# The third load of x goes from SyncE's queue to ScalarE's, ahead of two small vectors

## The chip, the cores and the metric

The kernel runs on one core of a Trainium2 chip. A core has five engines with a program each: TensorE (PE, with PEld for its weight loads), VectorE (DVE), ScalarE (ACT), GpSimd (POOL) and SyncE (SP). Engines that issue transfers do so in the order of their own program, and an issue can wait, which holds up all that stands behind it on that engine. The transfers themselves run on 16 DMA engines of the core. The metric is the device time of one execution in microseconds (us); lower is better.

## The reference

The input x has 2048 tokens of 1024 values. Three things are computed from it:

```python
g = sigmoid((x * gate_w).sum(-1, keepdims=True))          # a gate for each token
X = rfft2(x) * (w_r + 1j * w_i);  a = irfft2(X)           # a filter in the frequency domain
dt = exp(log_dt);  Lam_bar = exp(dt * (Lambda_re + 1j * Lambda_im))
Bu = x @ (((Lam_bar - 1) / Lam)[:, None] * (B_re + 1j * B_im)).T
h[t] = Lam_bar * h[t - 1] + Bu[t]                         # a complex scan over all 2048 tokens
b = 2 * (h @ (C_re + 1j * C_im).T).real + x * Dskip
out = g * a + (1 - g) * b
```

The five vectors Lambda_re, Lambda_im, log_dt, Dskip and gate_w have 1024 values each (2 KB). The first three are needed for the scan's coefficients, Dskip and gate_w later.

## The kernel before, in words

Everything is one program with its order written out by hand. The stages are generators (one for each kind of step), and a long string, `ORDER`, names a generator per letter: the program is emitted by stepping the generators in that order, and each engine runs its own instructions in the order in which they were emitted. Nothing is rearranged afterwards.

**Loads.** x is viewed as 128 partitions by 16 row groups of 1024 values and lands in the storage that later holds the matrix C (tile `CT`; `xn[i]` is its i-th part, with two row groups). `load_x` (letter `x`, line 242) makes the first two row groups two loads of 256 KB, called a and b below, and then one load of 512 KB for each further pair: c (row groups 2 and 3, i = 1), d, e, f and g; the last four row groups come by transposing loads (line 238). All of these are issued by SyncE, and so are the tables: `G` in three pieces (line 252, the matrices of the first Fourier step), `T2` in three pieces (line 247, those of the second), `JP` (line 1027), and the matrix B by transposing loads (line 259, letter `b`, tile `BT`). SyncE's order at the start is: a, b, c, the three pieces of G, d, two pieces of T2, e, JP, f, a transpose of B, g, a transposing load of x, and so on. The five small vectors are loaded at the very start by ScalarE on its own queue (line 211), into the rows of one tile, `vec8`.

**Completion semaphores.** The loads that SyncE and ScalarE issue take their completion semaphores in turn from a set of eight, in the order of emission over both queues. A load that gets a semaphore waits, on the engine that issues it, until the load that had it before has landed. So the ninth load waits for the first, and a load on one queue can wait for one on the other.

**What uses the first loads.** TensorE starts with seven idle matmuls on zeros (line 987), then transposes the row groups one after the other, eight 128 x 128 transposes each (`turn`, line 919, out of `CT` into a PSUM tile `pt`). The first three small vectors are turned between the first and the second row group (`turn_vectors`, line 1080). Ahead of row group 2, the first of load c, stand 22 filler transposes of the identity (line 917, `FILL_T`). Behind row group 2 stand the two late vectors (`turn_late_vectors`, line 1097), then row group 3, then the first matmuls of the Fourier step (`fd`, lines 433 and 443, against `G`). ScalarE copies each transposed row group to `xQ` (`turn_out`, line 929). Before its first copy it loads its function table; it then works out the coefficients of the scan (lines 1086 to 1113), takes over the late vectors (lines 1099 and 1100), and goes on with copies of row groups and of Fourier results (line 449). The second Fourier step on TensorE is line 462 (against `T2`), and ScalarE takes its results at line 474. VectorE folds the copied row groups (lines 943 to 954) and makes tables for the scan. The products of x with B (line 398) feed the scan from about 30 us on.

Of the kernel before, what the change touches and what calls it, by code (L numbers as in the profile page):

```python
# [24 lines left out]
P = 128  # L25
# [117 lines left out]
def kernel(  # L143
# [17 lines left out]
    nc = tc.nc  # L161
# [45 lines left out]


    vec8 = tmp.tile([8, 5, P], BF16, name="vec8")
    for i, src in enumerate((B_Lambda_re, B_Lambda_im, B_log_dt, B_Dskip, gate_w)):  # L210
        nc.scalar.dma_start(out=vec8[:, i, :], in_=src.rearrange("(j p) -> j p", p=P))
    ident = cpool.tile([P, P], BF16, name="ident")
    make_identity(nc, ident)
# [11 lines left out]
    xn = [CT[i // 4][:, 2 * (i % 4):2 * (i % 4) + 2, :] for i in range(8)]  # L225
    x_v = x.rearrange("(p j) d -> p j d", j=16)
# [7 lines left out]
    def load_x():  # L234
        for i in range(8):
            if i >= NTURN // 2:
                g = i - NTURN // 2
                nc.sync.dma_start_transpose(out=xt[:, :, :, g].rearrange("p j d s -> p (j d) s"), in_=x_sg[g][:, NTURN * D:])
                yield
                continue  # L240
            for js in (slice(0, 1), slice(1, 2)) if i == 0 else (slice(0, 2),):
                nc.sync.dma_start(out=xn[i][:, js], in_=x_v[:, 2 * i + js.start:2 * i + js.stop, :])
                yield

    def load_T2():
# [916 lines left out]
    def once(f):  # L1162
# [5 lines left out]
        "V": turn_vectors(), "|": turn_late_vectors(), "T": turn(), "U": turn_out(), "f": fold(), "~": mirror(), "u": fold_odd(), "F": fd(), "E": fd_out(), "S": s1(), "A": s1_out(), "1": s1_store(),  # L1168
        "K": keep_A1(), "h": unit_mm(), "H": unit_out(), "t": chain(*(make_tab(jp) for jp in range(4))), "r": radii(), "a": small(),
        "g": once(gate), "e": gate_out(), "b": load_B(), "c": load_C(), "2": load_T2(), "x": load_x(), "G": load_G(), "w": load_Wcols(), "k": load_turns(),  # L1170
        "n": early_mm(), "N": early_out(), "J": early_store(), "s": middle(), "L": load_small(), "M": load_mid(), "W": load_W(),
        "3": s2(), "4": s2_out(), "j": unit_cols(), "5": times_w(), "6": is1(), "7": is1_out(), "8": is1_store(), "q": load_last(), "i": is2(), "I": is2_out(),
# [43 lines left out]
```

## Time and profile before

| | |
|---|---|
| Time, median of 3 runs | 305.36 us (305.14 to 306.62) |
| The profiled execution's own time | 305.35 us |
| Its span in the profile | 303.6 us |
| Busy: TensorE / VectorE / ScalarE / GpSimd | 98% / 95% / 62% / 24% |
| Mean granted TensorE clock | 0.999 of full speed |

A row of a timeline has the start in us from the span's start, the length in us, the engine, the line, the operation, the tiles written and read, and xN for N merged instructions; square brackets tell how long the engine was idle before it and what ended that. SPq and ACTq are the queues of SyncE and ScalarE: their rows are the issuing of transfers, not the transfers. A row of waits has the waiting engine and line, what it waited for, the time in total, how often, and the longest. In the DMA view q1 is SyncE's queue and q10 ScalarE's. A row of windows has for each engine (PE, PEld, DVE, ACT, POOL) the busy time in that stretch, then the granted clock, the mean busy share of the DMA engines and GB/s.

### The profile page before, as it was taken

What the parts mean: (1) busy time and instruction counts of PE and PEld (TensorE: products, weight loads), DVE (VectorE), ACT (ScalarE), POOL (GpSimd) and SP (SyncE); (2) the same over time, 40 slices, a digit from 0 to 9 for tenths busy, and PEclk for the clock granted to TensorE, in tenths of its full rate; (3) what the DMA queues carried; (4) which work ended last, traced back from release to release, by engine and by line L of the source; (5) the groups of instructions that cost most, each with busy time, mean ns of one, the idle gap of its engine ahead of it and who ended that gap; (6) DMA issues with size and microseconds to landing.
All of it is one profiled execution on the core that took longest, in us unless ns stands there. A gap on an engine that the chain in (4) does not pass through costs nothing. (4 is left out here: it accounts for less than half of the span.)

```text
span 303.6 us, 6402 instructions
## 1 busy us (share of the span) xinstructions
PE 296.4 (98%) x2568; PEld 197.4 (65%) x2592; DVE 289.3 (95%) x340; ACT 188.5 (62%) x255; POOL 73.3 (24%) x99
## 2 busy tenths in 40 slices
PE   8999999999999999999999999999999999999995
PEld 5664677878864685458553866669657986645543
DVE  2999999999999999999999999999899999999995
ACT  4999999896532383667665865529668774343400
POOL 2100420745893001110210220202011253252330
PEclk9999999999999999999999999999999999999999
DMA  6999999989999599895948798687758876978976
GB/s 208 341 201 194 253 193 310 162 142 154 268 214 241 160 259 219 181 250 189 212 96 258 163 223 225 139 294 147 242 174 185 165 88 135 160 132 143 165 153 181
DMA packets 74157, 59.35 MB, mean 196 GB/s; under 512 B 44904, under 2 KB 61680, under 8 KB 74128
## 3 DMA queue, kind: packets, MB, share of 16 engines
q1 hardware_dynamic: 66560, 49.82, 65.8%
q0 software_dynamic: 6912, 8.69, 23.0%
q10 hardware_dynamic: 656, 0.44, 0.5%
q8 instruction: 20, 0.33, 0.4%
q14 instruction: 9, 0.07, 0.1%
HBM read 27.46 MB, written 23.08 MB: 166 GB/s over the span
## 5 line engine op out<-in xcount | busy, mean ns | idle before, releaser
L398 PE MATMUL psu<-xQ,BT 128*128 128x256 bf16 x1024 | 116.5, 273 | 0.2 <-DVE X L449 0.2
L398 PEld LDWEIGHTS <-BT 128*128 128x128 bf16 x1024 | 99.0, 98 | 17.3 <-issue 4.6
L713 PE MATMUL ps_y<-CT,h 128*128 128x512 bf16 x397 | 92.5, 379 | 0.9
L363 DVE TENSOR_TENSOR_SCAN h<-rz,h 128x2048 bf16<-128x2048 f32 (+1 forms) x20 | 70.8, 3561 | 0.0
L713 PEld LDWEIGHTS <-h 128*128 128x128 bf16 x416 | 39.6, 98 | 46.3 <-issue 2.9
L785 POOL DMA_DIRECT2D y_scratch<-su x20 | 17.3, 902 | 135.7 <-ACT su L779 105.4
L408 ACT CAST h<-psu 128x1024 bf16<-128x1024 f32 x32 | 32.3, 1011 | 18.7 <-PE psu L398 13.1
L350 DVE TENSOR_TENSOR h<-h,tab 128x4096 bf16<-128x4096 bf16 (+1 forms) x20 | 37.1, 1859 | 0.1
L744 ACT ACTIVATE ye<-ps_y,omg 128x512 f32<-128x512 f32 x26 | 17.9, 689 | 26.3 <-PE ps_y L713 11.8
L347 DVE TENSOR_TENSOR xQ<-h,tab 128x4096 bf16<-128x4096 bf16 x12 | 27.4, 2284 | 1.0 <-ACT h L408 1.0
L603 ACT CAST X<-ps_s 128x1024 bf16<-128x1024 f32 x16 | 16.2, 1010 | 14.6 <-PE ps_s L594 11.2
L727 PE MATMUL ps_q<-CT,h 128*128 128x512 bf16 (+2 forms) x110 | 21.3, 348 | 0.2
L817 ACT ACTIVATE BT<-ps_id,gB 128x1024 bf16<-128x1024 f32 x14 | 15.3, 1114 | 9.9 <-PE ps_id L810 5.7
L671 ACT CAST ZT<-ps_is 128x1024 bf16<-128x1024 f32 x16 | 15.8, 1017 | 6.2 <-PE ps_is L661 6.2
L637 ACT CAST C<-ps_is 128x1024 bf16<-128x1024 f32 x16 | 15.7, 1011 | 5.1 <-DMA xQ<-in_A_x_dram 3.4
L851 POOL DMA_DIRECT2D BT<-y_scratch x10 | 13.1, 1452 | 19.7 <-DVE BT L846 13.3
L727 PEld LDWEIGHTS <-h 128*128 128x128 bf16 x112 | 10.3, 98 | 10.4 <-DVE h L378 0.5
L779 ACT ACTIVATE su<-xs,omg 128x512 f32<-128x512 bf16 x20 | 14.2, 723 | 4.1 <-DMA y_scratch<-su 2.2
L929 ACT COPY xQ<-pt 128x1024 bf16<-128x1024 bf16 x12 | 12.2, 1082 | 1.3 <-PE pt L919 1.3
L449 ACT CAST X<-ps_fd 128x1024 bf16<-128x1024 f32 x12 | 12.3, 1062 | 1.0 <-PE ps_fd L439 0.9
L617 DVE TENSOR_TENSOR UV<-X,Wb 128x2048 bf16<-128x2048 bf16 x8 | 9.6, 1220 | 0.6 <-ACT ye L744 0.6
L617 DVE TENSOR_TENSOR UV<-X,raw 128x2048 bf16<-128x2048 bf16 x8 | 9.8, 1223 | 0.2 <-ACT X L604 0.2
(200 smaller groups left out, 397.3 us busy)
## 6 DMA issues: line engine op xcount, KB each, us to landing
y_scratch<-ye SPq DMA_DIRECT2D x20, 256.0 KB, 4.6
y_scratch<-su POOLq DMA_DIRECT2D x20, 256.0 KB, 4.7
Bb<-turn_scratch SPq DMA_DIRECT2D x16, 256.0 KB, 5.2
turn_scratch<-C SPq DMA_DIRECT2D x16, 256.0 KB, 4.1
raw<-turn_scratch SPq DMA_DIRECT2D x8, 512.0 KB, 4.3
xs<-in_A_x_dram SPq DMA_DIRECT2D x13, 256.0 KB, 3.9
out_dram<-BT SPq DMA_DIRECT2D x11, 256.0 KB, 4.3
CT<-in_A_x_dram SPq DMA_DIRECT2D x5, 512.0 KB, 6.1
```

The source lines that it names most:

```text
L347: nc.vector.tensor_mul(out=tmps["s"], in0=u[:, ::-1], in1=bc(i))
L350: nc.vector.tensor_mul(out=u, in0=u, in1=bc(i))
L363: nc.vector.tensor_tensor_scan(out=seg, data0=rz[:, js.start + j:js.start + j + m].rearrange("p j t -> p (j t)"), data1=seg, initial=0.0, ...
L398: nc.tensor.matmul(psu[:, j, :], lhsT=BT[4 * q + j][:, ri, d8, :], rhs=xQ[:, c, d8, :], start=(d8 == 0), stop=(d8 == 7))
L408: nc.scalar.copy(out=hs[c][:, ri, 4 * q:4 * q + 4].rearrange("p b (q j) -> p b q j", j=32), in_=psus.pop((c, q, ri)).rearrange("p b (j q) ...
L603: nc.scalar.copy(out=X2, in_=ps2s[g][b])
L617: nc.vector.tensor_mul(out=UV, in0=X2s.pop((g, b)).unsqueeze(1).to_broadcast([P, 2, 2, K]), in1=fft["Wb"][g // 2 % 2][:, :, at:at + 1, :]. ...
L671: nc.scalar.copy(out=ZT[:, 4 * kp:4 * kp + 4, :, 4 * G:4 * G + 4].rearrange("p (c r) n g -> p c r n g", c=2), in_=pszs.pop((G, kp)).rearra ...
L713: nc.tensor.matmul(psy, lhsT=hs[c][:, ri, jb, P * tq:P * (tq + 1)], rhs=CT[ri][:, jb, 512 * dh:512 * (dh + 1)], start=(i == 0), stop=(i == ...
L727: nc.tensor.matmul(psq, lhsT=hs[c][:, ri, jb, P * tq:P * (tq + 1)], rhs=CT[ri][:, jb, at:at + n], start=(i == 0), stop=(i == 15))
L744: nc.scalar.activation(out=ye, in_=psys[tb][:, K * hf:K * (hf + 1)], func=ACT.Copy, scale=omg[:, tb:tb + 1])
L785: nc.gpsimd.dma_start(out=y_dram[tb, hf], in_=xgs[tb, hf], accum_op=ALU.add)
```

## The change

Load c (row groups 2 and 3) is issued by ScalarE. It stands after Lambda_re, Lambda_im and log_dt, and the loads of Dskip and gate_w, which were issued directly after these, now follow load c. All loads have the same sources, destinations and sizes. ScalarE's order at the start is: Lambda_re, Lambda_im, log_dt, load c, Dskip, gate_w, the table load; SyncE's is: a, b, the three pieces of G, d, and on as before.

Because load c and the two vectors change places in the order of emission, the turns of the eight semaphores shift for the first loads: Dskip now waits for Lambda_re and gate_w for Lambda_im; the second piece of G waits for nothing and the third for load a; d waits for b and the first piece of T2 for log_dt, as before; the second piece of T2 waits for load c (Dskip before), e for the first piece of G (c before), JP for the second piece of G (gate_w before), f for Dskip (the first piece of G before), the first transpose of B for the third piece of G (the second before), and g for gate_w (the third piece of G before). From there on the waits are as they were.

```diff
     vec8 = tmp.tile([8, 5, P], BF16, name="vec8")
-    for i, src in enumerate((B_Lambda_re, B_Lambda_im, B_log_dt, B_Dskip, gate_w)):
+    vecs = list(enumerate((B_Lambda_re, B_Lambda_im, B_log_dt, B_Dskip, gate_w)))
+    for i, src in vecs[:3]:
         nc.scalar.dma_start(out=vec8[:, i, :], in_=src.rearrange("(j p) -> j p", p=P))
...
             for js in (slice(0, 1), slice(1, 2)) if i == 0 else (slice(0, 2),):
-                nc.sync.dma_start(out=xn[i][:, js], in_=x_v[:, 2 * i + js.start:2 * i + js.stop, :])
+                (nc.scalar if i == 1 else nc.sync).dma_start(out=xn[i][:, js], in_=x_v[:, 2 * i + js.start:2 * i + js.stop, :])
+                if i == 1:
+                    for k, src in vecs[3:]:
+                        nc.scalar.dma_start(out=vec8[:, k, :], in_=src.rearrange("(j p) -> j p", p=P))
                 yield
```

## The prediction

> **What bounds the kernel now.** I read the page first, then the timelines of SyncE's queue, ScalarE and TensorE over the first 30 us, the waits of SyncE's queue, the DMA landings in narrow stretches, and the one-microsecond windows. The change touches only the first 12 us, so the question is what limits that stretch and what it hands on.
>
> ```profile
> span 303.6 us, 6402 instructions
> PE 296.4 (98%) x2568; PEld 197.4 (65%) x2592; DVE 289.3 (95%) x340; ACT 188.5 (62%) x255; POOL 73.3 (24%) x99
> ...
> ACT  4999999896532383667665865529668774343400
> ```
>
> Over the whole span TensorE (98%) and VectorE (95%) are both full, so a delay handed on from the start has little idle time in which to vanish: 7.2 us on TensorE, 14.3 us on VectorE. One slice of the digits is 7.6 us: ScalarE, only 62% busy on average, is full from 8 to 53 us. The first stage is ScalarE's. SyncE's queue (duration is the issue time, xN the merged issues):
>
> ```profile
> 0.73 1.34 SPq L242 DMA_DIRECT2D CT<-in_A_x_dram  x3
> 2.12 2.06 SPq L252 DMA_DIRECT2D G_sb<-c_G  x3
> 4.22 0.72 SPq L242 DMA_DIRECT2D CT<-in_A_x_dram  x1
> 4.98 2.09 SPq L247 DMA_DIRECT2D raw<-c_T  x2
> 7.75 0.33 SPq L242 DMA_DIRECT2D CT<-in_A_x_dram  x1
> ...
> 8.60 0.44 SPq L242 DMA_DIRECT2D CT<-in_A_x_dram  x1
> 9.23 1.83 SPq L259 DMA_TRANSPOSE BT<-in_B_B_re_dram  x1
> ...
> 11.11 0.58 SPq L242 DMA_DIRECT2D CT<-in_A_x_dram  x1
> ```
>
> In order: x loads a, b and c (c is the one that moves), three pieces of G, load d, two pieces of T2, load e, (JP), load f, a transpose of B, load g. Three waits break this queue:
>
> ```profile
> SPq L247 <- DMA vec<-in_B_Dskip_dram: 1.1, 1, 1.1
> SPq L252 <- DMA CT<-in_A_x_dram: 0.8, 1, 0.8
> SPq L242 <- DMA CT<-in_A_x_dram: 0.7, 1, 0.7
> ```
>
> All three come from the eight completion semaphores, which the loads of both queues take in turn. The second G piece waits for load a, the second T2 piece for Dskip, load e for load c. So the end of the 0.7 us wait, 7.75, is when load c has landed. Landings by issue (last number: us from issue to landing), for loads b, c and d:
>
> ```profile
> CT<-in_A_x_dram SPq DMA_DIRECT2D x1, 256.0 KB, 2.8
> ...
> CT<-in_A_x_dram SPq DMA_DIRECT2D x1, 512.0 KB, 6.1
> ...
> CT<-in_A_x_dram SPq DMA_DIRECT2D x1, 512.0 KB, 7.0
> ```
>
> Load c starts to issue at 1.64 or so (7.75 less 6.1). Now the engines that use it:
>
> ```profile
> 6.53 1.39 PE L917 MATMUL pt<-ident 128*128 128x128 bf16 x22
> 7.78 0.62 PE L919 MATMUL pt<-ident,CT 128*128 128x128 bf16 x8
> 8.33 0.20 PE L1097 MATMUL vps<-ident,vec 8*128 8x8 bf16 x2
> ...
> 9.94 0.59 PE L443 MATMUL ps_fd<-G_sb,preT 128*128 128x512 bf16 x2 [0.20 <-DMA G_sb<-c_G]
> ...
> 13.01 0.60 PE L433 MATMUL ps_fd<-G_sb,preT 128*128 128x256 bf16 x4 [0.29 <-ACT X L449]
> ...
> 14.40 1.04 PE L462 MATMUL ps_s<-X,raw 64*128 64x512 bf16 x8
> 15.75 0.61 PE L919 MATMUL pt<-ident,CT 128*128 128x128 bf16 x8 [0.31 <-ACT xQ L929]
> ```
>
> The 22 transposes of L917 are filler. They keep TensorE busy from 6.53 to 7.92, and the first transposes of load c start as they drain, at 7.78. Landing and filler end together. Right behind, in order, stand the two late vectors (L1097). ScalarE:
>
> ```profile
> 1.33 0.29 ACTq L211 DMA_DIRECT2D vec<-in_B_Lambda_im_dram  x1
> ...
> 2.00 0.32 ACTq L211 DMA_DIRECT2D vec<-in_B_Dskip_dram  x1
> 2.35 0.32 ACTq L211 DMA_DIRECT2D vec<-in_gate_w_dram  x1
> 2.70 1.28 ACT L929 ACT_TABLE_LOAD   x1 [2.70 <-issue]
> 5.27 1.01 ACT L929 COPY xQ<-pt 128x1024 bf16<-128x1024 bf16 x1 [1.28 <-PE pt L919]
> ...
> 9.80 0.14 ACT L1099 CAST vecF<-vps 128x8 f32<-128x8 bf16 x1
> ...
> 10.11 1.94 ACT L929 COPY xQ<-pt 128x1024 bf16<-128x1024 bf16 x2
> 11.91 1.96 ACT L449 CAST X<-ps_fd 128x1024 bf16<-128x1024 f32 x2
> ...
> 15.53 1.08 ACT L474 CAST CT<-ps_s 128x1024 bf16<-128x1024 f32 x1
> ```
>
> From 9.80 on ScalarE goes without a gap. It takes the late vectors 1.27 us after TensorE has them (8.53), so TensorE runs ahead of the engine that limits this stage.
>
> **The change, part by part.**
>
> *ScalarE's issues.* One issue is added, 0.32 (a vector's row) to 0.45 us (1.34/3, SyncE's x loads). After the three first vectors it starts at 2.00, where Dskip did, and ends near 2.45. Dskip and gate_w follow, and in the new order of the semaphores each waits: Dskip for Lambda_re, gate_w for Lambda_im. Behind gate_w stand the table load, then the first copy of x. The third G piece waits for the same Lambda_im today and starts at about 3.74 (4.18 less 0.44) with no wait listed, so Lambda_im lands by then. Hence gate_w issues between 2.8 and 3.74, and the table load (1.28, plus the 0.03 between issue and load) ends between 4.4 and 5.37. The first copy starts at 5.27, ended by TensorE's transposes. Cost: 0 to 0.10. I take 0.05. The cover is the 1.28 us idle ahead of that copy; were it gone, the whole lot, about 0.45 of issue and 0.9 of wait, would stand on ScalarE's path.
>
> *Load c.* It issues at 2.00 instead of 1.64, 0.36 later. With its old 6.1 us it lands at 8.1. With what load d took, 7.0, at 9.0. With what load b took, 2.8, at 4.8. I take 8.1, since the size and the other loads in flight are load c's own; both ends stay for the rivals. An earlier landing earns TensorE nothing, because the filler holds it until 7.78 either way. Landing at 8.1 costs TensorE 0.35 there. TensorE has 0.20 at 9.94 (the G piece), 0.29 at 13.01 and 0.31 at 15.75 of waiting for others, and ScalarE's 1.27 stands behind. So 0.35 is hidden: 0 on the path. Without that cover it would be 0.35.
>
> *Dskip and gate_w* now stand behind 512 KB in their queue. They are used at 8.33 plus that 0.35, after the eight transposes of load c, 0.55 us behind them; if they land within 0.55 of load c they cost nothing. ScalarE starts to wait only when TensorE finishes L1097 after 9.80, that is from a landing at about 9.6. I take 0.
>
> *SyncE's queue.* The issue of load c, 0.45, leaves it: the first G piece goes at 1.64 instead of 2.12, the second needs no wait now and goes at 2.1 instead of 3.37, the third waits for load a (landed 3.37), load d for load b (1.19 plus 2.8 is 4.0) instead of 4.22. Later waits get worse: the second T2 piece waits for load c (8.1 instead of 6.75, +1.35), load e for the first G piece, load f for Dskip, the transpose of B for the third G piece, load g for gate_w. The G pieces are in by 8.60 to 9.94 today, so I put these four 0.7 to 1.0 later. What hides it: the queue already issued is deep. Load e, issued at 8.5, lands at 14.6 if it takes load c's 6.1 us, and its transposes run at 15.75. Load g:
>
> ```profile
> 18.64 0.24 POOL L1040 COPY Wp<-CT 128x64 bf16<-128x64 bf16 x1 [9.73 <-DMA CT<-in_A_x_dram]
> ...
> 20.78 0.61 PE L919 MATMUL pt<-ident,CT 128*128 128x128 bf16 x8
> ...
> PEld L398 <- DMA BT<-in_B_B_im_dram: 0.5, 2, 0.3
> ```
>
> GpSimd's wait shows load g in at 18.6; its transposes on TensorE are at 20.8, 2 us later. Of what stands behind these in the queue, only the B transposes show as waited for by TensorE, 0.5 us in two places. The bounds are minus 0.5 (these waits go) and plus 1.35 (the whole delay comes through). I take 0.
>
> Whether bandwidth is won can be read in the DMA rows of two stretches (GB/s is the last number), and in the queues from 5 to 7 us:
>
> ```profile
> 5.00:6.00 1.00, 1.00 (x11) 0.61 (x9) 0.00 (x0) 0.73 (x1) 0.00 (x0) 1.00 0.84 261
> 6.00:7.00 1.00, 1.00 (x18) 1.00 (x18) 0.94 (x6) 0.55 (x3) 0.48 (x2) 1.00 0.75 190
> ...
> q1 hardware_dynamic: 191, 0.45, 78.7%
> q10 hardware_dynamic: 16, 0.00, 0.7%
> ```
>
> The 16 engines have idle shares of 0.16 and 0.25 there, 0.41 us in all: what a second queue could fill. The few small packets of ScalarE's queue (q10) wait among those of SyncE's (q1): Dskip, 2 KB, issued at 2.00, landed only at 6.75. The Trainium skill speaks against a gain: "DMA: Bandwidth & Descriptors", section "Issuing engines are not separate DMA queues", says that loads from different issuing engines run on the same 16 engines and interleave, so that a second issuer saves only its issue time. Dskip's 4.75 us agree. By that rule the sum would be the 0.45 us of SyncE's issue at best, off the path here; by the idle 0.41 it would be about the same.
>
> **Sum.** 0.05 (table load) + 0 + 0 + 0 on a profiled execution of 305.35 us (303.6 span and 1.75 around it), which lies 0.01 below the median of 305.36: 305.4 us.
>
> **Rivals.**
>
> *A, slower: load c and its tail come late.* The place is L919 and L1097 on TensorE. If packets of the two queues alternate, each 4 KB of load c lets one 2 to 2.5 KB packet of G pass: 128 packets, 0.29 MB, at the 190 to 261 GB/s above 1.1 to 1.5 us. Load c lands at 9.4, and if the vectors behind it take 1.1 us more (the wait that Dskip causes today), L1097 runs at 10.5, 2.2 late. TensorE's waits give back 0.49 up to 13.01, so L462 is 1.7 late, and ScalarE, which takes it at 15.53 just after its end at 15.44, 1.6. That gives 305.35 + 1.6 = 307.0; both vectors paying 1.1 apart would give 308. It decides from a landing of gate_w at 9.6. For it: the wait on Dskip. Against: in load c's place in SyncE's queue G already follows, so the bytes ahead are few. The round robin between queues, packet by packet, is what "DMA: Bandwidth & Descriptors", section "Queues, rings and completion order", of the Trainium skill states; no row here shows two large loads sharing at this place. Chance 0.30.
>
> *B, faster: the front moves up.* Load c takes 2.8 us as load b did. The second T2 piece goes at 5.6 instead of 6.75 and all behind it up to 1.15 earlier; with the 0.5 of B waits gone that is 1.65: 303.7. For it: idle engines from 5 to 7. Against: the filler, and ScalarE without a gap. Chance 0.17.
>
> *C, SyncE's queue slips.* The whole 1.35 comes through at the B transposes: 306.7. Against: landings 1.1 to 2 us ahead of use. Chance 0.06, half of it beyond the bound.
>
> *The forecast* (the load moves, and nothing that matters notices) has 0.47, its own range 304.7 to 306.4.
>
> **How the numbers follow.** I say 0.5% (1.5 us) is about what this kernel's measurement can tell from no change. Faster 0.17 (B), same 0.50 (0.47 and half of C), slower 0.33 (A and half of C). The range runs from 303.5, just below B, to 308.0, the end of A.
>
> **What would show it.** In the changed profile: the table load ends by 5.4 and the first copy starts within 0.1 of 5.27; load c's first transposes start between 7.8 and 8.3; L1097 by 9.6, and ScalarE's L1099 still near 9.8; the second T2 piece is issued when load c has landed, and TensorE's wait for B stays under 1 us. I am wrong if L1097 stands beyond 9.6 with ScalarE idle ahead of L1099 (A), or if ScalarE's rows from 10 us on stand over 1 us earlier (B).

## The result, and the profile after

The changed kernel takes 306.70 us (median of 20 runs, 305.94 to 307.98) where the kernel before takes 305.21 (20 runs, 304.44 to 306.90). The ratio is 1.0048, with a 95% interval of 1.0034 to 1.0062: 1.5 us slower. That is a real difference, and its size lies just inside the 0.5% that the prediction counted as no change. The profiled execution took 307.53 us, with a span of 305.7; it is one of the longer of its kind, so what its rows add up to (2.1 us of span more than before) is more than the median lost.

In the changed kernel every line number from `load_x` on is 1 higher and, from the T2 load on, 4 higher than before: the copy L925 is now L929, the transposes L919 are L923, the products L398 are L402.

The busy times of the page of the changed kernel:

```profile
span 305.7 us, 6403 instructions
PE 296.4 (97%) x2568; PEld 197.2 (64%) x2592; DVE 289.7 (95%) x340; ACT 188.5 (62%) x255; POOL 71.0 (23%) x99
```

No engine does more work than before (TensorE 296.4 both times, VectorE 0.4 more). The 2.1 us are waiting. SyncE's queue in the changed kernel:

```profile
4.86 4.58 SPq L251 DMA_DIRECT2D raw<-c_T  x2
9.49 0.43 SPq L243 DMA_DIRECT2D CT<-in_A_x_dram  x1
...
10.91 1.80 SPq L263 DMA_TRANSPOSE BT<-in_B_B_re_dram  x1
12.76 0.75 SPq L243 DMA_DIRECT2D CT<-in_A_x_dram  x1
...
21.59 3.23 SPq L239 DMA_TRANSPOSE CT<-in_A_x_dram  x1
```

Up to 4.9 us the queue is where it was or a little ahead of it (load d goes at 4.07 for 4.22). Then the row of the two T2 pieces is 4.58 long: the second piece waits inside it. In the waits of SyncE's queue and in the DMA issues of the changed kernel this reads:

```profile
SPq L251 <- DMA CT<-in_A_x_dram: 3.6, 1, 3.6
...
CT<-in_A_x_dram ACTq DMA_DIRECT2D x1, 512.0 KB, 7.1
G_sb<-c_G SPq DMA_DIRECT2D x2, 256.0 KB, 7.2
```

Load c, issued by ScalarE at 2.01, took 7.1 us and landed at 9.1. Load e, right behind the second T2 piece, is issued at 9.49 instead of 7.75, the first transpose of B at 10.91 instead of 9.23, load g at 12.76 instead of 11.11. Behind load g come the two transposing loads of x (row groups 12 to 15). The second of them went out like this before; set it against 21.59 above:

```profile
19.76 2.94 SPq L238 DMA_TRANSPOSE CT<-in_A_x_dram  x1
```

Up to there everything behind the wait is 1.6 to 1.9 us late, and the queue does not win that back: its last two transposes of B go 2.35 late (49.05 for 46.70). Now ScalarE of the changed kernel:

```profile
3.64 0.28 ACTq L246 DMA_DIRECT2D vec<-in_gate_w_dram  x1
3.95 1.28 ACT L933 ACT_TABLE_LOAD   x1 [3.95 <-DMA vec<-in_B_Lambda_im_dram]
5.27 1.01 ACT L933 COPY xQ<-pt 128x1024 bf16<-128x1024 bf16 x1
...
10.00 0.14 ACT L1103 CAST vecF<-vps 128x8 f32<-128x8 bf16 x1
15.83 1.02 ACT L478 CAST CT<-ps_s 128x1024 bf16<-128x1024 f32 x1
...
27.76 3.88 ACT L929 COPY xQ<-CT 128x1024 bf16<-128x1024 bf16 x4 [1.69 <-DMA CT<-in_A_x_dram]
```

The first copy starts as before to the hundredth (5.27), the late vectors come 0.20 later (10.00 for 9.80), the first results of the second Fourier step 0.30 later (15.83 for 15.53). Then, at 26 us, stands a wait that was not there: 1.69 us for the transposing loads of x. Before, this copy followed the one ahead of it without a gap:

```profile
25.51 4.03 ACT L925 COPY xQ<-CT 128x1024 bf16<-128x1024 bf16 x4
```

TensorE of the changed kernel (the last row's xN depends on the stretch that was asked for):

```profile
9.15 0.62 PE L923 MATMUL pt<-ident,CT 128*128 128x128 bf16 x8 [1.35 <-DMA CT<-in_A_x_dram]
9.71 0.20 PE L1101 MATMUL vps<-ident,vec 8*128 8x8 bf16 x2
...
15.19 1.04 PE L466 MATMUL ps_s<-X,raw 64*128 64x512 bf16 x8
...
31.70 3.65 PE L402 MATMUL psu<-xQ,BT 128*128 128x256 bf16 x32 [1.15 <-ACT xQ L929]
...
50.55 1.91 PE L402 MATMUL psu<-xQ,BT 128*128 128x256 bf16 x16
52.94 5.29 PE L402 MATMUL psu<-xQ,BT 128*128 128x256 bf16 x45 [0.48 <-DMA BT<-in_B_B_im_dram]
```

and the same two stages before:

```profile
30.33 3.65 PE L398 MATMUL psu<-xQ,BT 128*128 128x256 bf16 x32 [0.19 <-DVE X L449]
...
48.93 9.33 PE L398 MATMUL psu<-xQ,BT 128*128 128x256 bf16 x81
```

ScalarE was 0.56 late when it began to wait for these loads (26.07 for 25.51); the copy then starts when they land, so that this lateness is contained in the wait and not added to it.

There are three new waits on TensorE: 1.35 for load c at 9.15, 1.15 for ScalarE's copy of row groups 12 to 15 at 31.70, and 0.48 for the B transposes at 52.94. Of the first, 0.79 us is left at L466 (15.19 for 14.40) and 0.41 at the transposes of row group 6, the first of load e (16.16 for 15.75). With the second, the products that begin at 50.55 are 1.62 late (48.93 before); with the third, 2.10. The span is 2.1 longer. So on balance nothing after 53 us adds to it or takes from it. What the rows do not say is which of the first two waits is the cause: both lie ahead of the products, and load c is the one that moved.

### The profile page after: what moved, and what is told of

It reads as the page before. It is cut to its first block, busy times and chain, and to the rows that moved or that the text cites. A ratio compares the mean times of both kernels' runs of the same rounds, so it can differ in the third digit from the quotient of the medians.

```text
span 305.7 us, 6403 instructions
## 1 busy us (share of the span) xinstructions
PE 296.4 (97%) x2568; PEld 197.2 (64%) x2592; DVE 289.7 (95%) x340; ACT 188.5 (62%) x255; POOL 71.0 (23%) x99
## 3 DMA queue, kind: packets, MB, share of 16 engines
q1 hardware_dynamic: 66416, 49.30, 65.8%
## 5 line engine op out<-in xcount | busy, mean ns | idle before, releaser
L402 PE MATMUL psu<-xQ,BT 128*128 128x256 bf16 x1024 | 116.5, 273 | 1.8 <-ACT xQ L929 1.1
L402 PEld LDWEIGHTS <-BT 128*128 128x128 bf16 x1024 | 99.1, 98 | 19.0 <-issue 5.9
L821 ACT ACTIVATE BT<-ps_id,gB 128x1024 bf16<-128x1024 f32 x14 | 15.3, 1114 | 10.4 <-PE ps_id L814 5.7
L731 PEld LDWEIGHTS <-h 128*128 128x128 bf16 x112 | 10.3, 98 | 10.5 <-DVE h L382 0.5
```

Of the source, the lines that this page charges most:

```text
L402: nc.tensor.matmul(psu[:, j, :], lhsT=BT[4 * q + j][:, ri, d8, :], rhs=xQ[:, c, d8, :], start=(d8 == 0), stop=(d8 == 7))
L731: nc.tensor.matmul(psq, lhsT=hs[c][:, ri, jb, P * tq:P * (tq + 1)], rhs=CT[ri][:, jb, at:at + n], start=(i == 0), stop=(i == 15))
```

## The experiments

Three theories. **T**: TensorE's stall before load c (1.35 us) and ScalarE's late vectors behind it are handed on to the end. **S**: SyncE's queue is the cause; the second T2 piece waits for load c's semaphore, all loads behind it slip, and TensorE's stall costs nothing. **R**, inside S: what is paid is the lateness of row groups 12 to 15 alone, at ScalarE's L929. In the quoted expectations S is called theory Q. The rival to R, called theory B there, is that the B transposes behind take the same lateness.

**Hold SyncE's queue in the kernel before.** Load c stays on SyncE. A write by GpSimd into the place of the second T2 piece makes that piece wait until about 9 us (`HOLD` is 960):

```diff
             nc.gpsimd.memset(rz[:, jb, 0:1], 0.0)
+            if jb == 1:
+                nc.gpsimd.memset(raw[:, 384:384 + HOLD], 0.0)
             yield
```

> The kernel before with one addition: GpSimd clears the place of the second T2 piece at about 8.3 to 9.2 us, so that SyncE issues this piece at about 9.2 instead of 6.75, as late as in the changed kernel (9.12). Load c stays on SyncE and TensorE's first transposes of it stay near 7.8. Theory Q (SyncE's queue slips behind the wait for load c; rival C): load e at about 9.5, ScalarE waits 1.2 to 2.0 us ahead of the last row groups (L925 of the kernel before), 1.0 to 1.6 us slower than before. Theory T (TensorE's stall before load c costs the time; rival A): no change, within 0.3 us.

Measured: 306.43 us (10 runs) against 305.28 (31 runs), ratio 1.0044 [1.0013, 1.0076]. The median is 1.15 us slower, with load c where it was. The profile of this kernel, SyncE, TensorE and ScalarE:

```profile
9.40 0.43 SPq L243 DMA_DIRECT2D CT<-in_A_x_dram  x1
...
20.07 2.85 SPq L239 DMA_TRANSPOSE CT<-in_A_x_dram  x1
...
7.36 0.61 PE L922 MATMUL pt<-ident,CT 128*128 128x128 bf16 x8
...
26.20 3.88 ACT L928 COPY xQ<-CT 128x1024 bf16<-128x1024 bf16 x4 [0.57 <-DMA CT<-in_A_x_dram]
```

Load e goes at 9.40, nearly where the changed kernel has it (9.49), and TensorE has load c at 7.36 without a stall: S without T. The execution that was profiled, however, was the fastest of the ten (305.38). In it the queue won its lateness back: 1.65 late at load e (9.40 for 7.75), 0.31 at the second transposing load of x (20.07 for 19.76), and ScalarE's wait is only 0.57. The expected wait of the changed kernel's size is not in this trace; the times say that the hold costs, this trace does not show where.

**TensorE's stall alone, in the kernel before.** 24 more filler transposes keep TensorE from load c until 8.2 us. Nothing is done to any queue:

```diff
-FILL_T = {2: 22}
+FILL_T = {2: 46}
```

> The kernel before with 46 filler transposes instead of 22 ahead of load c: 24 more at 58 ns hold TensorE 1.4 us longer, so that load c's transposes start at about 9.15 as in the changed kernel, while no load moves. Theory T: 1.2 to 1.5 us slower. Theory Q: the stall is hidden behind ScalarE, 0 to 0.4 us slower, and ScalarE's L1099 at about 10.0.

Measured: 305.56 us, ratio 1.0000 [0.9981, 1.0019].

```profile
4.07 0.61 PE L919 MATMUL pt<-ident,CT 128*128 128x128 bf16 x8
...
5.64 2.73 PE L917 MATMUL pt<-ident 128*128 128x128 bf16 x46
8.21 0.61 PE L919 MATMUL pt<-ident,CT 128*128 128x128 bf16 x8
```

TensorE spends 1.34 us more on filler (2.73 for 1.39) and the time does not move. The delay against the kernel before is smaller than meant in this execution, 0.43 (8.21 for 7.78), because its first transposes ran faster (last section), and for the same reason ScalarE takes the late vectors at 9.16 and not at the expected 10.0. So this run alone speaks weakly against T. The next one is stronger.

**The changed kernel without most of the slip.** The late vectors go through GpSimd's queue instead of ScalarE's. They then take no turn among the eight semaphores of SyncE's and ScalarE's loads, and the load that waits for load c is JP, two loads later; load c itself stays on ScalarE:

```diff
                 if i == 1:
                     for k, src in vecs[3:]:
-                        nc.scalar.dma_start(out=vec8[:, k, :], ...)
+                        nc.gpsimd.dma_start(out=vec8[:, k, :], ...)
```

> The changed kernel, but Dskip and gate_w are issued by GpSimd, whose loads take no turn of the eight semaphores. Load c stays on ScalarE after three vectors. The second T2 piece then waits for load b and load e for log_dt, so SyncE issues both by about 6; the first wait for load c falls on JP. Theory Q: load e at 5.5 to 6, most of the slip gone as far as the queue behind JP is not late; ScalarE's wait before the last row groups under 1.0 us, and the time within 0.7 us of before. Theory T: load c still lands at about 9, TensorE still stalls about 1.3 us, 1.2 to 1.5 us slower than before.

Measured: 305.49 us (10 runs), ratio 1.0002 [0.9981, 1.0023]. The loss is gone.

```profile
5.95 0.71 SPq L243 DMA_DIRECT2D CT<-in_A_x_dram  x1
9.16 0.32 SPq L1031 DMA_DIRECT2D JP_sb<-c_JP  x1
...
20.26 2.35 SPq L239 DMA_TRANSPOSE CT<-in_A_x_dram  x1
...
9.19 0.62 PE L923 MATMUL pt<-ident,CT 128*128 128x128 bf16 x8 [1.39 <-DMA CT<-in_A_x_dram]
...
9.98 0.17 ACT L1103 CAST vecF<-vps 128x8 f32<-128x8 bf16 x1
25.95 3.91 ACT L929 COPY xQ<-CT 128x1024 bf16<-128x1024 bf16 x4
```

This is the changed kernel as far as TensorE goes: load c at 9.19 after a stall of 1.39, late vectors at 9.98. But load e goes at 5.95, ahead of the wait, the second transposing load of x at 20.26 instead of 21.59, and ScalarE's copy has no wait. Some of the slip is left behind JP (20.26 is 0.50 later than before). T expects the loss to stay; it went. The windows from 9 to 11 us show what the slip left undone, before, after and here (DMA share and GB/s are the last two numbers):

```profile
9.00:11.00 2.00, 1.80 (x14) 1.19 (x13) 1.97 (x13) 1.99 (x6) 0.00 (x0) 1.00 1.04 406
```
```profile
9.00:11.00 2.00, 1.85 (x23) 1.56 (x25) 1.97 (x12) 1.99 (x6) 0.00 (x0) 1.00 0.78 256
```
```profile
9.00:11.00 2.00, 1.81 (x23) 1.52 (x25) 1.97 (x13) 1.90 (x6) 0.00 (x0) 1.00 1.05 408
```

In the changed kernel the DMA engines ran partly empty there (256 GB/s for 406), since what should have run had not been issued.

**An earlier queue.** The vectors as in the run above, but load c back on SyncE:

```diff
-    for i, src in enumerate((B_Lambda_re, B_Lambda_im, B_log_dt, B_Dskip, gate_w)):
+    vecs = list(enumerate((B_Lambda_re, B_Lambda_im, B_log_dt, B_Dskip, gate_w)))
+    for i, src in vecs[:3]:
...
                 nc.sync.dma_start(out=xn[i][:, js], ...)
+                if i == 1:
+                    for k, src in vecs[3:]:
+                        nc.gpsimd.dma_start(out=vec8[:, k, :], ...)
```

> The kernel before, load c on SyncE, but Dskip and gate_w are issued by GpSimd. The second T2 piece then waits for load b and load e for log_dt, so SyncE issues both by about 6 instead of 6.75 and 7.75; JP waits for load c. Theory Q: SyncE's front moves up and the last row groups land earlier; 0 to 0.8 us faster than before, if GpSimd's vectors land by 8.3. Theory T: load c lands at 7.7 as before, no change.

Measured: 305.29 us, ratio 0.9996 [0.9977, 1.0015]. Load e goes at 6.09, 1.66 earlier than before, and nothing is won. By load g the lead is gone again (11.30 for 11.11). So this queue's lateness costs, and its earliness up to load e earns nothing. The execution in the trace took 306.05, 0.76 above the median, and it waits for B, as the changed kernel does, though its queue was not held up:

```profile
51.90 6.33 PE L402 MATMUL psu<-xQ,BT 128*128 128x256 bf16 x55 [0.85 <-DMA BT<-in_B_B_im_dram]
```

**Where it is paid.** In the changed kernel, load g and the two transposing loads of x are put ahead of the first two B transposes in the written order:

```diff
-    "...TTEUfffUFbxwxbxbbTUEFbfE",
+    "...TTEUfffUFxwxxbbbbTUEFbfE",
```

> The changed kernel, but on SyncE load g and the two transposing loads of x (row groups 12 to 15) go ahead of the first two transposes of B; nothing else moves. Theory R (the slip of SyncE's queue is paid where ScalarE waits for row groups 12 to 15, 1.7 us in the changed kernel): the wait ahead of ScalarE's L929 at about 26 us falls under 0.3 us, TensorE's 1.1 us wait for that copy goes, 0.9 to 1.5 us faster than the changed kernel, within 0.7 us of before. Theory B (it is paid at the transposes of B, as rival C had it): these land no earlier, TensorE's wait for B at L402 grows over 1.6 us, and the time stays 1.0 us or more over before.

Measured: 307.00 us (12 runs) against 305.25 (35 runs), ratio 1.0060 [1.0035, 1.0085]. No gain over the changed kernel. The profile, ScalarE and TensorE:

```profile
25.90 4.02 ACT L929 COPY xQ<-CT 128x1024 bf16<-128x1024 bf16 x4
...
49.32 1.91 PE L402 MATMUL psu<-xQ,BT 128*128 128x256 bf16 x16
52.64 5.61 PE L402 MATMUL psu<-xQ,BT 128*128 128x256 bf16 x48 [1.40 <-DMA BT<-in_B_B_im_dram]
```

The copy of row groups 12 to 15 has no wait any more, and the products at 49.32 are only 0.39 late; then 1.40 is lost at the B transposes. The 0.39 is not the queue's: ScalarE's table load waits until 4.45 here, its first copy starts at 5.75 instead of 5.27, and 0.39 of that is still there at 10.19 (the late vectors, 9.80 before) and at 25.90. The time is theory B's, its wait of over 1.6 is not quite reached. So R alone fails. The same edit to the kernel before:

```diff
-    "...TTEUfffUFbxwxbxbbTUEFbfE",
+    "...TTEUfffUFxwxxbbbbTUEFbfE",
```

> The kernel before with the same move: load g and the transposing loads of x ahead of the first two transposes of B. ScalarE does not wait for these loads in the kernel before, so theory R expects no change, within 0.4 us, and theory B expects it slower by up to 0.5 us if the first transposes of B land after 30 us.

gave 305.04 us, ratio 0.9995 [0.9983, 1.0007]: the order by itself is free. A wait for B stands in its trace too. The last two transposes of B on SyncE's queue and TensorE's row, in this kernel and then in the changed kernel with the same order:

```profile
47.39 2.79 SPq L259 DMA_TRANSPOSE BT<-in_B_B_im_dram  x2
...
51.27 6.92 PE L398 MATMUL psu<-xQ,BT 128*128 128x256 bf16 x61 [0.44 <-DMA BT<-in_B_B_im_dram]
```
```profile
48.66 2.85 SPq L263 DMA_TRANSPOSE BT<-in_B_B_im_dram  x2
```

With the slip they go 1.27 later, and the wait is 1.40 instead of 0.44. So about 1 us of it is the slip's, and the rest is there without it. The lateness is a debt of the whole queue: with row groups 12 to 15 out of its way it is paid at the next load that is needed with no time to spare.

**A longer hold.** Two of the writes by GpSimd in the kernel before:

```diff
             if jb == 1:
-                nc.gpsimd.memset(raw[:, 384:384 + HOLD], 0.0)
+                for _ in range(2):
+                    nc.gpsimd.memset(raw[:, 384:384 + HOLD], 0.0)
```

> As the run that held the second T2 piece, but GpSimd clears its place twice, so that SyncE issues it at about 10.0 instead of 9.2. If a late SyncE queue alone sets the loss, each further 0.8 to 0.9 us costs about as much: 1.7 to 2.4 us slower than before, with ScalarE waiting 1.3 us or more before the last row groups. If the loss of the first hold had another cause (GpSimd's own work), the time stays near the 1.15 us of that run.

Measured: 306.35 us (12 runs) against 305.25, ratio 1.0029 [1.0014, 1.0044]. Slower again with load c on SyncE, but not by more than with one write: 1.10 us by the medians, below the expected size, with overlapping intervals. By the time alone that is what the expectation gave to the other cause, GpSimd's own work. The profile speaks for the queue, and shows what the first hold's did not:

```profile
10.49 0.43 SPq L243 DMA_DIRECT2D CT<-in_A_x_dram  x1
...
27.48 3.88 ACT L929 COPY xQ<-CT 128x1024 bf16<-128x1024 bf16 x4 [1.71 <-DMA CT<-in_A_x_dram]
...
50.26 8.00 PE L402 MATMUL psu<-xQ,BT 128*128 128x256 bf16 x69
```

Load e is 2.74 late, ScalarE waits 1.71 at the same place as in the changed kernel, and the products at 50.26 are 1.33 late with no wait for B; the span is 304.9, 1.3 longer than before. This is the changed kernel's first payment, without its load on ScalarE's queue and without its stall (load c is transposed at 8.08, with no wait). In the first 60 us no engine but SyncE, which is meant to, waits for GpSimd longer than in the kernel before.

**Both remedies.** The changed kernel with the vectors on GpSimd and the new order:

```diff
-                        nc.scalar.dma_start(out=vec8[:, k, :], ...)
+                        nc.gpsimd.dma_start(out=vec8[:, k, :], ...)
...
-    "...TTEUfffUFbxwxbxbbTUEFbfE",
+    "...TTEUfffUFxwxxbbbbTUEFbfE",
```

> Load c on ScalarE, Dskip and gate_w on GpSimd, and the transposing loads of x ahead of the first two transposes of B. Theory R: no wait of ScalarE for row groups 12 to 15 is left, TensorE still stalls about 1.4 us before load c; 305.0 to 305.6, no gain over the kernel before, since ScalarE is full from 7 us on in either.

Measured: 304.98 us, ratio 0.9990 [0.9975, 1.0005]. No clear gain over the kernel before. ScalarE has no wait for row groups 12 to 15 in the trace (its copy starts at 25.88), and TensorE's stall before load c is 1.41.

**The changed kernel and its remedy again, side by side on one chip**, both without a further edit.

> The changed kernel again, beside the next two on the same chip. Both theories: 1.0035 to 1.0062 of the kernel before; TensorE's first transposes of load c at about 9.15, the second T2 piece at about 9.1.

> The changed kernel with Dskip and gate_w issued by GpSimd, again. Theory Q (the loss is the slip of SyncE's queue, paid by TensorE at about 30 and 51 us): TensorE still stalls 1.4 us before load c, yet the time is within 0.25% of before and 0.2 to 0.6% under the changed kernel beside it. Theory T (the stall before load c is the loss): as slow as the changed kernel.

Measured: the changed kernel 307.93 us (12 runs), ratio 1.0055 [1.0030, 1.0081]; with the vectors on GpSimd 305.98 (12 runs), ratio 1.0000 [0.9975, 1.0025], against 305.47 (29 runs). The quotients of these medians are larger than the ratios on record, 1.0081 and 1.0017; I compare by the ratios, whose intervals lie just apart. The profile of the changed kernel's execution here:

```profile
8.67 0.62 PE L923 MATMUL pt<-ident,CT 128*128 128x128 bf16 x8 [0.32 <-DMA CT<-in_A_x_dram]
...
27.43 2.94 ACT L929 COPY xQ<-CT 128x1024 bf16<-128x1024 bf16 x3 [1.42 <-DMA CT<-in_A_x_dram]
...
50.22 1.91 PE L402 MATMUL psu<-xQ,BT 128*128 128x256 bf16 x16
53.30 4.97 PE L402 MATMUL psu<-xQ,BT 128*128 128x256 bf16 x43 [1.17 <-DMA BT<-in_B_B_im_dram]
```

Load c landed sooner than expected here (the second T2 piece goes at 8.64, not at about 9.1), the stall before it is only 0.32, and the execution took 307.75 us all the same. ScalarE's wait at L929 and the wait for B are both there. This is not quite S without T: TensorE's filler ended later here, and load c's transposes are still 0.89 later than in the kernel before (8.67 for 7.78). The other kernel's execution has the whole of T and little of S:

```profile
9.08 0.62 PE L923 MATMUL pt<-ident,CT 128*128 128x128 bf16 x8 [1.43 <-DMA CT<-in_A_x_dram]
...
49.27 1.91 PE L402 MATMUL psu<-xQ,BT 128*128 128x256 bf16 x16
52.74 5.47 PE L402 MATMUL psu<-xQ,BT 128*128 128x256 bf16 x47 [1.57 <-DMA BT<-in_B_B_im_dram]
```

It was one of the slowest of its kind (306.93; they range from 304.80 to 307.26), and not by the stall, which leaves it 0.34 late at 49.27, but by a wait of 1.57 for B. SyncE's queue was late after all there, though not from the start: three transposes of B at 36.46 took 5.61 us to issue (4.00 in the first execution of this kernel), and the last two went at 48.69 instead of 47.42.

**Load c first of all on ScalarE's queue**, ahead of the small vectors, in a version of the kernel before with the two late vectors on GpSimd:

```diff
+    nc.scalar.dma_start(out=CT[0][:, 2:4, :], in_=x.rearrange("(p j) d -> p j d", j=16)[:, 2:4, :])
...
-        nc.scalar.dma_start(out=vec8[:, i, :], ...)
+        (nc.scalar if i < 3 else nc.gpsimd).dma_start(out=vec8[:, i, :], ...)
...
+                if i != 1:
+                    nc.sync.dma_start(out=xn[i][:, js], ...)
```

> Load c is ScalarE's very first issue, ahead of Lambda_re, Lambda_im and log_dt; Dskip and gate_w are issued by GpSimd. Load c should land at 6 to 7.5, before the filler ends, so TensorE has no stall there; loads a and b share the engines with it and may land 0.3 to 1 us later than before. Theory Q: no gain over the kernel before (304.9 to 305.8), since ScalarE sets the first stage; 0.3 to 0.8 us slower if the three first vectors come after 5.2. Theory T: the time is that of before, or lower by what is left of the filler's end.

Measured: 305.58 us, ratio 0.9985 [0.9960, 1.0010]: no change. Load c is in time now, earlier than expected (issued at 0.72, 4.3 us to landing), but load a is late by its company: the transposes of the first row group wait 0.53 us at 4.91, and the wait for Lambda_im adds 0.42 at 6.06. The early landing is paid for by its neighbours. The expectation gave 0.3 to 0.8 us of loss to vectors that come after 5.2; they did, ScalarE took the late vectors 0.89 later than before (10.69 for 9.80), and no loss shows in the time.

**The two payments put together.** From the rows above, the products that begin near 49 us measure the lateness brought from before, and the wait right behind them is that for B. Against the kernel before (48.93, no wait, span 303.6), for the one execution of each run that was profiled:

| kernel | starts at | late by | wait for B | sum | span longer by |
|---|---|---|---|---|---|
| changed kernel | 50.55 | 1.62 | 0.48 | 2.10 | 2.1 |
| changed kernel again | 50.22 | 1.29 | 1.17 | 2.46 | 2.4 |
| changed, x loads ahead of B | 49.32 | 0.39 | 1.40 | 1.79 | 1.8 |
| before, longer hold | 50.26 | 1.33 | none | 1.33 | 1.3 |
| before, hold | 48.99 | 0.06 | none | 0.06 | 0.0 |
| changed, vectors on GpSimd | 49.38 | 0.45 | none | 0.45 | 0.0 |
| the same again | 49.27 | 0.34 | 1.57 | 1.91 | 1.5 |
| both remedies | 49.30 | 0.37 | none | 0.37 | -0.4 |
| load c first on ScalarE | 49.83 | 0.90 | none | 0.90 | 0.2 |
| before, vectors on GpSimd | 49.13 | 0.20 | 0.85 | 1.05 | 0.7 |
| before, x loads ahead of B | 48.93 | 0.00 | 0.44 | 0.44 | 0.3 |
| before, more filler | 48.38 | -0.55 | 0.35 | -0.20 | -0.2 |

In the first five rows, where the queue was held up at the start, the two add up to the span's growth within 0.1. In the others up to 0.8 us is given back later. The wait for B is not the slip's alone: it stands in three traces without any slip made (0.35 to 0.85), and it comes and goes (none, 1.57) between two executions of one kernel whose median is that of before. It follows when SyncE issues the last two transposes of B: in six of the seven traces with this wait, TensorE goes on 3.9 to 4.2 us after that issue (4.8 in the changed kernel again).

## Why the prediction was right, and where it was not

The forecast was 305.4 in a range of 303.5 to 308.0, most likely within 0.5%. The measured 306.7, 0.48% over the kernel before, lies in the range and just within that bound. But it lies outside the forecast's own 304.7 to 306.4, and it is the number of rival C (306.7, chance 0.06), by what C starts from, the slip of SyncE's queue. That the forecast of no change holds is luck, by the narrowest margin. That C's number was met is partly luck too, since neither its place nor its size is what the runs showed.

*The sum's table load, 0.05.* Right in the first trace: load and first copy stand at 3.95 and 5.27. gate_w did wait for Lambda_im and was issued at 3.64, inside the 2.8 to 3.74 that was worked out; the 1.28 of idle time covered it. It does not always: in the changed kernel again the first copy starts at 5.39, and with the x loads ahead of B at 5.75, beyond the bound of 0.10. Where ScalarE waits for the transposing loads, at 26 us, that disappears in the wait.

*Load c.* Taken to land at 8.1 with a bound of 9.0; it landed at 9.1. The late issue (0.36) was right, the old 6.1 us of landing time was not: it took 7.1. TensorE's stall was 1.35 instead of 0.35. That this is hidden was right nonetheless: the runs with the stall and without most of the slip cost nothing (1.0002 and 1.0000).

*Late vectors, 0.* Right in cost. L1101 ran at 9.71, 0.11 beyond the 9.6 from which rival A was to decide, and ScalarE took the vectors 0.20 late. But that is not A: ScalarE has no idle time ahead of them, and it was 0.20 late already at 8.15 (line 1114, 7.95 before), ahead of TensorE's turn of the vectors. A's price, 307.0, is near the measured time by chance. With 9.98 for the vectors in the kernel with GpSimd's queue, the loss was gone.

*SyncE's queue, "I take 0".* This is the step that failed. The waits were listed rightly, one by one, and so was the sign of the slip; its size was 1.74 at load e instead of the 0.7 to 1.0 used there, as load c landed a microsecond later than taken. The cover was what was wrong. It was checked for loads e and g, which were in time indeed (TensorE shows no wait for either). For the rest the prediction looked at TensorE's waits alone ("only the B transposes show as waited for by TensorE"), and the transposing loads of row groups 12 to 15, whose reader is ScalarE, were passed over; the trace of before shows no wait for them. A load that is waited for 0 us can be one that lands with nothing to spare. These were: with the second one issued at 19.76 ScalarE's copy started on time at 25.51, with 20.07 (the hold) it waited 0.57, with 21.59 it waited 1.69. In the five traces in which ScalarE waits, the copy starts 5.7 to 6.2 us after that issue; the trace of before had 5.75 (25.51 less 19.76), so little or nothing to spare. With the vectors on GpSimd 20.26 was in time for a copy at 25.95, while 20.17 in the second execution cost 0.28. So the step that failed is the cover, and what stands in its place is no slack at row groups 12 to 15 and at the B transposes.

*Rival B* (the front moves up, 303.7) fell, and more than by the late landing: with load e issued 1.66 earlier nothing was gained. The 0.41 us of idle DMA time that spoke for it is doubtful as well: the share reads 1.04 from 9 to 11 us, so what it lacks to 1 need not be idle time. *Rival C* named the B transposes as the place and 1.35 as the most. The place is two, row groups 12 to 15 and B, and the sum is 1.8 to 2.5 in the three traces of the changed kernel, with either order.

Open: the price of the slip is not proportional to it (holds to 9.4 and 10.5 us at load e cost 1.15 and 1.10), and the one trace of the shorter hold shows the queue catching up rather than the loss. Why the queue wins time back or loses it among the transposes was not settled, and the wait for B, from 0 to 1.57, hangs on that. In the last set of runs 9 of the 29 executions of the kernel before also took 306.4 to 307.2 us; none of these was traced, so whether they wait for B is not known.

## What to carry to other kernels

A load that changes queue takes its turn at the completion semaphores with it, and the load that next needs that semaphore may sit on a queue that had nothing to do with it: list who waits for whom under the new order, and price the wait with the moved load's worst landing time, not its old one. Then follow every load behind that wait to its first consumer, and measure the slack as the consumer's start less the landing; a load that shows no wait may have none left. Look at every engine's waits, not at those of the busiest alone. Here a stall of up to 1.4 us on TensorE, which runs ahead of ScalarE in this stage, cost nothing that could be measured.

## What the runs showed of the hardware

*Landing times when two queues carry large loads.* Load c took 7.1 us on ScalarE's queue against 6.1 on SyncE's, and the two 256 KB pieces of G beside it 7.2 in the median against 5.8. Issued first of all on ScalarE's queue load c took 4.3, and loads a and b beside it 4.3 instead of 2.7. So the second queue made the neighbours slower each time. That agrees with the Trainium skill, "DMA: Bandwidth & Descriptors", section "Issuing engines are not separate DMA queues", by which loads of different issuing engines run on the same 16 DMA engines and interleave. That the sharing alone is the cause was not isolated: the loads are also issued at other times.

*The first transposes.* The first eight transposes took 1.06 us in the kernel before and 0.61 in the execution with more filler, though nothing ahead of them differs:

```profile
4.17 1.06 PE L919 MATMUL pt<-ident,CT 128*128 128x128 bf16 x8
```

The granted clock reads 9 tenths or more in the first slice of the page in both, and 1.00 in the windows of one microsecond from 4 to 6 us, so no row shows the clock as the cause. What follows stood about half a microsecond earlier in that execution, which is as much as some of the effects looked for here. The Trainium skill, "TensorE: Matmul & The Clock Gate", section "Part 1: The HAM clock gate", says that the window in which activity is counted runs freely, so that the step up to the full clock varies by 500 ns either way. The 0.45 us between the two rows are of that size, which is all that can be said here.
